# A gated linear recurrence with an ELU feed-forward layer: the state held per head and multiplied in four 64x64 quadrants

## The chip, the cores and the metric

The kernel runs on one core of a Trainium2 chip. The metric is the device time of one execution in microseconds (us). TensorE multiplies matrices into PSUM (eight banks of 512 fp32 columns on 128 partitions), VectorE and ScalarE work on SBUF and PSUM, GpSimd on SBUF alone, and SyncE (SP) issues the transfers. In the rows TensorE's matmuls are PE, its loads of the stationary operand PEld, VectorE DVE, ScalarE ACT and GpSimd POOL.

## The reference

Four sequences of 768 tokens, eight heads of 48 channels. A recurrence over tokens gives y; its heads side by side are x (3072 tokens, 384 channels), and two matrices with an ELU between them follow. Everything is fp32.

```python
B, H, S, D = r.shape                                  # 4, 8, 768, 48
for t in range(S):
    cur = np.einsum('bhd,bhe->bhde', u[None] * kt, vt)
    y[:, :, t] = np.einsum('bhd,bhde->bhe', rt, state + cur)
    state = w[None, :, :, None] * state + np.einsum('bhd,bhe->bhde', kt, vt)
x = y.transpose(0, 2, 1, 3).reshape(B * S, H * D)     # 3072 x 384
h = x @ w_in                                          # 384 x 2048
g = np.where(h > 0.0, h, np.exp(np.minimum(h, 0.0)) - 1.0)
out = g @ w_out                                       # 2048 x 384
```

## The kernel before

**Tiling.** The tokens of each sequence are cut into six chunks n of 128 (NCH). A unit is one (n, b), b being the sequence. The recurrence becomes matmuls per unit: the scores of the unit's tokens against each other for each head, masked; these by v; and the state left by the chunks before, by r. The state of b is then decayed and the chunk's k by v is added. Layer n is the feed-forward part for the 512 tokens of chunk n (all four b): 16 steps f, each with a hidden product (`hidden`, L939, 9 matmuls of 512 columns: three channel chunks by three products of high and low parts), the ELU over ScalarE and VectorE (L948, L949, L954), a split into high and low parts (L960, L962) and a projection of an earlier step (`project`, L976, 12 matmuls of 384 columns). The feed-forward products use fp32r operands, the recurrence fp32.

**Heads on partitions.** r and k, with channels on partitions, hold two heads on 128 partitions: the even head at rows 0 to 47, the odd one at 64 to 111 (ROWS), the other rows are padding. H / 2 = 4 such pairs a lie side by side (HP). `state[b]` has for each pair a 128x128 block of which only two 48x48 blocks, on the diagonal, are not zero.

**Order.** The order of the work is written out by hand and kept: START lists the start (chunk 0 and the first weights), FIRST the operations of one step of layer 0, LATER those of a step of layers 1 to 5. An operation's digit names the stage of the unit that it serves; a unit takes four steps. Layer 0 carries the units of chunk 1, layers 1 to 4 those of chunks 2 to 5, and layer 0 also prepares the weights (split into high and low parts on ScalarE, VectorE and GpSimd, L519 to L558). In layer 0 r and k are turned by TensorE (L567, then L621 on VectorE); from layer 1 on by VectorE's 32x32 transposes (L579) and two trips through DRAM (L588, L593), with L609 on GpSimd.

**What one unit does around the change.** `scores` (A, L692): 8 matmuls per head in row halves of the array (48 rows, 128 columns), odd and even heads into two banks, copied through a mask on VectorE by `take_scores` (L718). One step later `outputs` (Y): four state matmuls over whole pairs (L796, 128x128), eight matmuls of v by scores in column halves (L804, 64 columns), all into one bank y; right behind them `added_state` (L820), eight matmuls k by v of 48x48 into a second bank. `split_x` (xh on ScalarE, L847; xl on VectorE, L849) splits y into high and low parts: three of the four pairs go to x, the fourth to a tile `fill`, and `fill_x` (G, L858) moves its rows by six transfers into the padding rows of x, so that the 384 channels fill three chunks of 128. `new_state` (ns, L834) adds the added state to the decayed one, `decay_state` (sw on GpSimd, swd on VectorE in layer 0, L677) makes that decayed state, with one instruction for each half of the rows. PSUM: in the steps four banks hold the projection's sums, two the hidden product, and two in turn (tag rw) scores, y and added state.

**Channels.** Because of the padding x's channels are in another order than the reference's; `load_weights` (L212, L213) reads the rows of w_in in that same order, by two transfers for rows 0 to 47 and 64 to 111 and two for the padding rows. `x_tokens` (L763) and `turn_out` do the same for chunk 0, where y is computed with tokens on partitions.

Of the kernel before, what the change touches and what calls it, by code (L numbers as in the profile page):

```python
# [17 lines left out]
P = 128  # L18
B, H, S, D = 4, 8, 768, 48
DP = 64  # L20
# [6 lines left out]
X = 2 * NC * T  # L27

ROWS = [slice(i * DP, i * DP + D) for i in range(2)]
HALVES = [(rows, slice(None), rows) for rows in ROWS]  # L30


PAIR = 2 * D
REST = NC * PAIR
# [30 lines left out]
class Kernel:  # L65
# [7 lines left out]
    def prepare(self, ctx):  # L73
# [4 lines left out]
        self.state = [cp.tile([P, HP, P], F32, tag=f"state{b}", name=f"state{b}") for b in range(B)]  # L78
# [121 lines left out]
    def load_weights(self, j):  # L200
# [4 lines left out]
        if j % 2 == 0:  # L205

            st = st.rearrange("p (c f) t -> p c (f t)", c=NC)
            cols = slice(f * 2 * P, (f + 1) * 2 * P)
            pairs = self.w_in[0:REST, cols].rearrange("(c i p) f -> i p c f", c=NC, i=2)
            fill = self.w_in[REST:DM, cols].rearrange("(i c p) f -> i p c f", c=NC, i=2)  # L210
            for i in range(2):
                nc.sync.dma_start(st[ROWS[i]], pairs[i])  # L212
                nc.sync.dma_start(st[FILLS[i]], fill[i])  # L213
        else:
            nc.sync.dma_start(
                st.rearrange("p f t -> p (f t)"), self.w_out[f * P : (f + 1) * P, :]
            )
# [259 lines left out]
    def inverse_table(self):  # L477

        nc, wk = self.nc, self.wk
        near = wk.tile([P, HP, 16], F32, tag="near", name="near")  # L480
        far = wk.tile([P, HP, 8], F32, tag="far", name="far")
# [189 lines left out]
    def decay_state(self, n, b, eng=None):  # L671
# [4 lines left out]
        for at in HALVES:  # L676
            (eng or self.nc.gpsimd).tensor_mul(  # L677
                un["sw"][at[0]], self.state[b][at],
                self.pw[at[0], :, P : P + 1].to_broadcast([D, HP, D]),
            )  # L680
# [71 lines left out]
    def x_tokens(self, n, b):  # L752
# [5 lines left out]
        for part, at, form in (  # L758
            (slice(0, REST), slice(0, D), "p (c i d) -> p c i d"),
            (slice(REST, DM), slice(D, DP), "p (i c d) -> p c i d"),  # L760
        ):
            y_part, vd_part = (t[:, part].rearrange(form, c=NC, i=2) for t in (y, vd))
            nc.vector.tensor_add(x[:, :, :, at], y_part, vd_part)  # L763
# [10 lines left out]
    def x_of(self, n):  # L774
        if n not in self.x:
            self.x[n] = self.wk.tile(
                [P, 2, NC, T], F32R, tag="x", name="x", bufs=1 if self.general else 2
# [3 lines left out]
    def split_turned(self, n, b, i):  # L781
        nc, px = self.nc, self.units[n, b]["px"]
        x = self.x_of(n)[:, :, :, b * P : (b + 1) * P]
# [29 lines left out]
    def added_state(self, n, b):  # L813
# [4 lines left out]
        pst = self.bank("st")  # L818
        for h in range(H):
            nc.tensor.matmul(  # L820
                pst[ROWS[h % 2], (h // 2) * D : (h // 2 + 1) * D],
                lhsT=kr[:, h, 0:D], rhs=v_t[:, h, :], start=True, stop=True,
# [3 lines left out]
    def new_state(self, n, b):  # L826
# [5 lines left out]
        for at in HALVES:  # L832
            if n > 0:
                nc.vector.tensor_add(self.state[b][at], un["sw"][at[0]], un["ps"][at[0]])  # L834
            else:
                nc.scalar.copy(self.state[b][at], un["ps"][at[0]])
# [200 lines left out]
```

## Time and profile before

| | us |
|---|---|
| median of 3 runs | 528.35 (525.35 to 531.41) |
| the profiled execution's time | 524.89 |
| its span, first to last instruction | 523.1 |
| TensorE matmuls busy in the span | 504.1 |
| VectorE busy | 289.0 |
| ScalarE busy | 243.5 |
| GpSimd busy | 168.0 |

The profiled execution's time is 1.8 us over its span; it lies below the lowest of the three runs. Times in rows are microseconds from the span's start unless marked ns; L796 is line 796 of the kernel. A row of the timeline merges neighbouring instructions of one kind (x8): its length runs from the first one's start to the last one's end, and matmuls overlap, so that the distance between the starts of two rows says when TensorE goes on.

### The profile page before, as it was taken

The page shows a single profiled execution, that of the slowest core. Times are in us where ns is not written, and L with a number is a line of the kernel's source. Part 1 is how long each engine was busy: PE and PEld are TensorE (multiplying, and loading weights), DVE is VectorE, ACT ScalarE, POOL GpSimd, SP SyncE. Part 2 cuts the span into 40 slices and gives each one's busy share as a digit, 9 for nine tenths or more (in the row PEclk, how much of TensorE's full clock was granted, in tenths as well). Part 3 has the DMA queues.
Part 4 walks back from the last instruction along what each step waited for, and adds up shares of the span by engine and source line. Part 5 has one row for each costly group of instructions (what it writes and reads, how often), then busy time and mean ns, then how long its engine had stood idle before and what let it go on. Part 6 is the DMA issues. An engine that isn't in the chain of part 4 may idle for free.

```text
span 523.1 us, 9010 instructions
## 1 busy us (share of the span) xinstructions
PE 504.1 (96%) x3380; PEld 450.3 (86%) x3380; DVE 289.0 (55%) x496; ACT 243.5 (47%) x429; POOL 168.0 (32%) x192
## 2 busy tenths in 40 slices
PE   6889999999999999999999999999999999999994
PEld 5879898987988988988988988989889889999994
DVE  6989999996454454454444644544543542433331
ACT  2289787775344333434334443333434344444441
POOL 6732233125524524525525435234133220000000
PEclk9999999999999999999999999999999999999999
DMA  9987858535624523543424354335245200100001
GB/s 138 210 184 186 174 149 218 127 63 138 146 69 83 117 66 68 130 136 64 124 53 94 99 132 97 86 56 127 84 111 129 71 25 9 59 3 0 1 0 67
DMA packets 105561, 50.89 MB, mean 97 GB/s; under 512 B 80162, under 2 KB 101412, under 8 KB 105508
## 3 DMA queue, kind: packets, MB, share of 16 engines
q1 hardware_dynamic: 105508, 50.23, 42.0%
q8 instruction: 28, 0.46, 0.4%
q14 instruction: 25, 0.20, 0.1%
HBM read 35.13 MB, written 13.11 MB: 92 GB/s over the span
## 4 chain that ended last, share of the span: by engine, by line
PE 82%; DVE 6%; SPq 4%; ACT 3%; DMA 2%; issue 1%; POOL 0%; ACTq 0%; DVEq 0%
PE ps_acc L976 35%; PE ps_h L939 34%; PE ps_a L692 4%; PE ps_y L804 4%; PE ps_y L796 3%; DVE wide L541 1%; SPq L167 1%; PE ps_st L820 1%; DVE wide L533 1%; DVE rk L621 1%; ACT stage L525 1%; DVE ps_h L954 1%; DMA x<-fill 1%; PE ps_y L747 1%; SPq L212 1%
## 5 line engine op out<-in xcount | busy, mean ns | idle before, releaser
L976 PE MATMUL ps_acc<-wh,g 128*128 128x384 f32 x768 | 216.0, 343 | 0.5 <-DVE g L962 0.5
L939 PE MATMUL ps_h<-x,wh 128*128 128x512 f32 (+1 forms) x588 | 181.1, 389 | 0.7 <-DMA x<-fill 0.7
L976 PEld LDWEIGHTS ps_acc<-wh,g 128*128 128x128 f32 x768 | 139.9, 188 | 7.1 <-DVE g L962 1.0
L954 DVE SCALAR_TENSOR_TENSOR ps_h<-g,ps_h 128x512 f32<-128x512 f32 x96 | 66.8, 695 | 133.3 <-ACT g L949 132.8
L976 PE MATMUL ps_acc<-wl,g 128*128 128x384 f32 x384 | 129.0, 336 | 0.0
L939 PEld LDWEIGHTS ps_h<-x,wh 128*128 128x128 f32 x588 | 108.5, 188 | 16.9 <-DMA x<-fill 1.0
L948 ACT ACTIVATE g<-ps_h 128x512 f32<-128x512 f32 x96 | 57.4, 598 | 136.9 <-PE ps_h L939 136.9
L939 PE MATMUL ps_h<-x,wl 128*128 128x512 f32 (+1 forms) x294 | 114.1, 388 | 0.0
L960 ACT CAST g<-ps_h 128x512 fp32r<-128x512 f32 x96 | 56.4, 587 | 82.6 <-DVE ps_h L954 82.2
L962 DVE TENSOR_TENSOR g<-ps_h,g 128x512 fp32r<-128x512 f32 x96 | 66.0, 688 | 36.1 <-ACT g L960 35.2
L976 PEld LDWEIGHTS ps_acc<-wl,g 128*128 128x128 f32 x384 | 72.3, 188 | 1.9
L711 POOL TENSOR_TENSOR a<-ident,diag 128x512 f32<-128x512 f32 x35 | 35.9, 1045 | 108.6 <-DVE diag L660 100.7
L939 PEld LDWEIGHTS ps_h<-x,wl 128*128 128x128 f32 x294 | 55.1, 188 | 13.7
L949 ACT ACTIVATE g<-g 128x512 f32<-128x512 f32 x96 | 60.7, 632 | 3.1
L667 POOL TENSOR_TENSOR k_t<-k_t,rev 128x384 f32<-128x384 f32 x16 | 16.2, 1012 | 62.6 <-DVE tb L579 49.9
L558 POOL TENSOR_TENSOR wl<-wide,wh 128x384 fp32r<-128x384 f32 x17 | 17.4, 1021 | 50.5 <-ACT wh L551 46.1
L849 DVE TENSOR_TENSOR fill<-ps_y,fill 128x128 fp32r<-128x128 f32 x20 | 5.8, 290 | 46.7 <-ACT x L847 46.7
L718 DVE COPY_PREDICATED a<-mask,ps_a 128x512 f32<-128x512 int32 x40 | 27.3, 736 | 0.0
L652 POOL TENSOR_TENSOR ru<-r_t,u_b 128x384 f32<-128x384 f32 x17 | 17.3, 1016 | 17.4 <-DMA r_t<-in_r_dram 14.9
L796 PEld LDWEIGHTS ps_y<-rk,state 128*128 128x128 f32 x160 | 20.9, 191 | 1.6
L804 PE MATMUL ps_y<-a,v_t 128*64 128x128 f32 x320 | 21.9, 279 | 0.0
L609 POOL TENSOR_TENSOR rk<-rk,pw 128x512 f32<-128x512 f32 x16 | 19.1, 1192 | 6.6 <-DMA rk<-blocks 6.6
(105 smaller groups left out, 440.1 us busy)
## 6 DMA issues: line engine op xcount, KB each, us to landing
blocks<-tb SPq DMA_DIRECT2D x64, 128.0 KB, 2.3
rk<-blocks SPq DMA_DIRECT2D x16, 512.0 KB, 3.6
stage<-in_moe_w_out_dram SPq DMA_DIRECT2D x16, 384.0 KB, 4.2
stage<-in_moe_w_in_dram SPq DMA_DIRECT2D x32, 144.0 KB, 4.2
out_dram<-stage SPq DMA_DIRECT2D x24, 192.0 KB, 3.3
r_t<-in_r_dram SPq DMA_DIRECT2D x22, 192.0 KB, 3.4
k_t<-in_k_dram SPq DMA_DIRECT2D x22, 192.0 KB, 3.9
v_t<-in_v_dram SPq DMA_DIRECT2D x22, 192.0 KB, 4.1
```

The source lines that it names most:

```text
L692: self.nc.tensor.matmul(pa[i][:, a * P : (a + 1) * P], lhsT=kw[rows, a, :], rhs=rw[rows, a, :], start=True, stop=True,)
L711: self.nc.gpsimd.tensor_mul(un["a"][i], self.ident.unsqueeze(1).to_broadcast([P, HP, P]), diag.unsqueeze(2).to_broadcast([P, HP, P]),)
L718: self.nc.vector.copy_predicated(un["a"][i], self.mask.bitcast(I32).unsqueeze(1).to_broadcast([P, HP, P]), un["pa"][i].rearrange("p (a t) ...
L796: nc.tensor.matmul(py[:, a * P : (a + 1) * P], lhsT=self.state[b][:, a, :], rhs=un["r"][:, a, :], start=(a == 0), stop=False, skip_group_c ...
L804: nc.tensor.matmul(py[i * DP : (i + 1) * DP, a * P : (a + 1) * P], lhsT=v[:, h * D : h * D + DP], rhs=un["a"][i][:, a, :], start=(n == 0 a ...
L939: self.nc.tensor.matmul(ph[:, part], lhsT=a[:, c * P : (c + 1) * P], rhs=x[:, c, part], start=(c == 0 and i == 0), stop=(c == NC - 1 and i ...
L948: nc.scalar.activation(g, ph, AF.Relu, scale=-1.0)
L949: nc.scalar.activation(g, g, AF.Exp, scale=-1.0)
L954: self.nc.vector.scalar_tensor_tensor(ph, g, -1.0, ph, op0=ALU.add, op1=ALU.max)
L960: nc.scalar.copy(part, g)
L962: nc.vector.tensor_sub(part, g, self.g[n, f][2].bitcast(F32))
L976: self.nc.tensor.matmul(self.acc[n][b][:, 0:DM], lhsT=a[:, at], rhs=w, start=(f == 0 and i == 0), stop=(f == NF - 1 and i == 2),)
```

## The change

- `state[b]` keeps for each pair the two 48x48 blocks only: the even head's on rows 0 to 47, the odd head's on rows 64 to 111, both in the same 64 columns. Decay, addition and copies address those columns; the decay is one instruction over all partitions.
- `outputs` multiplies the state per head: eight matmuls of 48 rows by 64 columns instead of four of 128x128. Even heads (i = 0) read rows 0 to 47 and write bank py[0], odd heads rows 64 to 111 and py[1]; c = 0 or 1 picks partitions 0 to 63 or 64 to 127 of the bank. Heads run in the order s, i, c, with h = 4c + 2s + i. The matmuls of v by scores take the same order.
- y stands in the first 256 columns of two banks. The added state of chunks 1 to 4 goes to the last 256 columns of py[0], no longer to a bank of its own.
- x's channel chunk k (k = 0 to 3) is head k on rows 0 to 63 and head 4 + k on rows 64 to 127; `split_x` copies two chunks from each bank, 256 columns at a time. The tile x has room for chunk 3, which took the tile `fill` before; `fill_x` reads it there. The rows of w_in, `x_tokens` and the split of chunk 0 follow that order. The tiles near and far of the start lie in the tile sw.

```diff
-        self.state = [cp.tile([P, HP, P], F32, tag=f"state{b}", name=f"state{b}") for b in range(B)]
+        self.state = [cp.tile([P, HP, DP], F32, tag=f"state{b}", name=f"state{b}") for b in range(B)]
...
-            pairs = self.w_in[0:REST, cols].rearrange("(c i p) f -> i p c f", c=NC, i=2)
-            fill = self.w_in[REST:DM, cols].rearrange("(i c p) f -> i p c f", c=NC, i=2)
+            heads = self.w_in[:, cols].rearrange("(i c p) f -> i p c f", i=2, p=D)
             for i in range(2):
-                nc.sync.dma_start(st[ROWS[i]], pairs[i])
-                nc.sync.dma_start(st[FILLS[i]], fill[i])
+                last = slice((i * HP + NC) * D, (i + 1) * HP * D)
+                fill = self.w_in[last, cols].rearrange("(c p) f -> p c f", c=NC)
+                nc.sync.dma_start(st[ROWS[i]], heads[i][:, 0:NC])
+                nc.sync.dma_start(st[FILLS[i]], fill)
...
         un["sw"] = self.wk.tile([P, HP, D], F32, tag="sw", name="sw", bufs=1)
-        for at in HALVES:
-            (eng or self.nc.gpsimd).tensor_mul(
-                un["sw"][at[0]], self.state[b][at],
-                self.pw[at[0], :, P : P + 1].to_broadcast([D, HP, D]),
-            )
+        (eng or self.nc.gpsimd).tensor_mul(
+            un["sw"], self.state[b][:, :, 0:D], self.pw[:, :, P : P + 1].to_broadcast([P, HP, D])
+        )
...
     def outputs(self, n, b):
         nc, un = self.nc, self.units[n, b]
         v = self.raw[n, b][2]
-        py = self.bank("y")
+        py = un["py"] = [self.bank("y") for _ in range(2)]
+        at = [
+            (4 * c + 2 * s + i, py[i][c * DP : (c + 1) * DP, s * P : (s + 1) * P], s)
+            for s in range(2) for i in range(2) for c in range(2)
+        ]
         if n > 0:
-            for a in range(HP):
+            for h, y, s in at:
+                rows, a = ROWS[h % 2], h // 2
                 nc.tensor.matmul(
-                    py[:, a * P : (a + 1) * P], lhsT=self.state[b][:, a, :], rhs=un["r"][:, a, :],
-                    start=(a == 0), stop=False, skip_group_check=True,
+                    y, lhsT=self.state[b][rows, a, :], rhs=un["r"][rows, a, :],
+                    start=(s == 0), stop=False, skip_group_check=True,
                 )
-        for h in range(H):
-            a, i = h // 2, h % 2
+        for h, y, s in at:
             nc.tensor.matmul(
-                py[i * DP : (i + 1) * DP, a * P : (a + 1) * P], lhsT=v[:, h * D : h * D + DP],
-                rhs=un["a"][i][:, a, :], start=(n == 0 and a == 0), stop=(a == HP - 1),
-                skip_group_check=True,
-            )
-        un["py"] = py.rearrange("p (c t) -> p c t", c=HP)
+                y, lhsT=v[:, h * D : h * D + DP], rhs=un["a"][h % 2][:, h // 2, :],
+                start=(n == 0 and s == 0), stop=(s == 1), skip_group_check=True,
+            )
...
-        pst = self.bank("st")
+        pst = (self.bank("st") if n == 0 else un["py"][0])[:, 2 * P :]
...
     def split_x(self, n, b, i):
         nc, un = self.nc, self.units[n, b]
-        if "fill" not in un:
-            un["fill"] = self.wk.tile([P, 2, P], F32R, tag="fill", name="fill", bufs=2)
-        x, fill, py = self.x_of(n)[:, :, :, b * P : (b + 1) * P], un["fill"], un["py"]
-        for hi, lo, y in (
-            (fill[:, 0], fill[:, 1], py[:, NC]), (x[:, 0], x[:, 1], py[:, 0:NC])
-        ):
+        for j, py in enumerate(un["py"]):
+            x = self.x_of(n)[:, :, j::2, b * P : (b + 1) * P]
+            y = py[:, 0 : 2 * P].rearrange("p (s t) -> p s t", s=2)
             if i == 0:
-                nc.scalar.copy(hi, y)
+                nc.scalar.copy(x[:, 0], y)
             else:
-                nc.vector.tensor_sub(lo, y, hi.bitcast(F32))
+                nc.vector.tensor_sub(x[:, 1], y, x[:, 0].bitcast(F32))
...
-                self.nc.sync.dma_start(x[FILLS[i], :, c], fill[rows])
+                self.nc.sync.dma_start(x[FILLS[i], :, c], x[rows, :, NC])
```

## Rows read from the trace of the kernel before

**Rows 1.** The page: TensorE's busy time, its 40 slices and its granted clock.
```profile
PE 504.1 (96%) x3380; PEld 450.3 (86%) x3380; DVE 289.0 (55%) x496; ACT 243.5 (47%) x429; POOL 168.0 (32%) x192
...
PE   6889999999999999999999999999999999999994
...
PEclk9999999999999999999999999999999999999999
```

**Rows 2.** Busy by stage: length, PE, PEld, DVE, ACT, POOL (instructions), clock, DMA, GB/s.
```profile
39.00:122.00 83.00, 78.94 (x555) 70.08 (x555) 76.25 (x126) 65.76 (x115) 24.10 (x24) 1.00 0.64 151
122.00:204.00 82.00, 82.00 (x561) 72.85 (x563) 40.91 (x71) 32.96 (x60) 37.66 (x41) 1.00 0.46 103
...
367.00:434.00 67.00, 67.00 (x428) 59.65 (x429) 30.52 (x51) 27.55 (x49) 17.56 (x16) 1.00 0.32 82
```

**Rows 3.** TensorE's waits from 38 us on: total us, times, longest.
```profile
PE ps_a L692 <- DVE rk L621: 4.0, 4, 1.3
...
PEld ps_a L692 <- issue: 4.9, 14, 0.4
```

**Rows 4.** Timeline of TensorE over a unit in layer 2: start, length, instruction, tiles.
```profile
223.85 0.39 PE L939 MATMUL ps_h<-x,wl 128*128 128x512 f32 x1
224.17 1.16 PE L692 MATMUL ps_a<-rk,tb 48*128 48x128 f32 x16
225.26 0.45 PE L976 MATMUL ps_acc<-wh,g 128*128 128x384 f32 x1
...
228.61 0.40 PE L939 MATMUL ps_h<-x,wl 128*128 128x512 f32 x1
...
229.30 0.39 PE L939 MATMUL ps_h<-x,wl 128*128 128x512 f32 x1
229.53 1.05 PE L796 MATMUL ps_y<-rk,state 128*128 128x128 f32 x8
230.51 1.09 PE L804 MATMUL ps_y<-a,v_t 128*64 128x128 f32 x16
231.44 0.53 PE L820 MATMUL ps_st<-v_t,k_t 128*48 128x48 f32 x16
...
244.58 0.38 PE L692 MATMUL ps_a<-rk,tb 48*128 48x128 f32 x2
```

**Rows 5.** TensorE's timeline in windows 224.165:224.178 and 230.512:230.530: records begun.
```profile
224.17 0.38 PE L692 MATMUL ps_a<-rk,tb 48*128 48x128 f32 x2
...
230.51 0.33 PE L804 MATMUL ps_y<-a,v_t 128*64 128x128 f32 x2
```

**Rows 6.** Groups by line and shape: count, busy us, mean ns, idle before, releasers.
```profile
L796 PE MATMUL ps_y<-rk,state 128*128 128x128 f32 x160 | 21.0, 274 | 0.0
...
L847 ACT CAST x<-ps_y 128x384 fp32r<-128x384 f32 x20 | 9.7, 486 | 0.0
...
L849 DVE TENSOR_TENSOR fill<-ps_y,fill 128x128 fp32r<-128x128 f32 x20 | 5.8, 290 | 46.7 <-ACT x L847 46.7
L847 ACT CAST fill<-ps_y 128x128 fp32r<-128x128 f32 x20 | 5.3, 266 | 16.3 <-PE ps_y L804 13.9 <-PE ps_st L820 2.3
...
L677 DVE TENSOR_TENSOR sw<-state,pw 48x192 f32<-48x192 f32 x8 | 3.3, 411 | 0.1
```

**Rows 7.** Timeline of a unit in layer 0, from its state product on.
```profile
66.76 1.05 PE L796 MATMUL ps_y<-rk,state 128*128 128x128 f32 x8
...
68.91 0.27 ACT L847 CAST fill<-ps_y 128x128 fp32r<-128x128 f32 x1 [1.25 <-PE ps_st L820]
...
70.75 0.70 DVE L954 SCALAR_TENSOR_TENSOR ps_h<-g,ps_h 128x512 f32<-128x512 f32 x1 [0.21 <-ACT g L949]
```

**Rows 8.** Timeline of the end of layer 0.
```profile
114.48 0.73 DVE L677 TENSOR_TENSOR sw<-state,pw 48x192 f32<-48x192 f32 x2
...
117.58 0.55 DVE L849 TENSOR_TENSOR x<-ps_y,x 128x384 fp32r<-128x384 f32 x1
...
121.97 0.73 PE L939 MATMUL ps_h<-x,wh 128*128 128x512 f32 x2 [0.73 <-DMA x<-fill]
```

More of the change, by code (lines that the diff above doesn't have):

```diff
@@ L26 @@
 T = B * P
-X = 2 * NC * T
+X = 2 * (NC + 1) * T
 ROWS = [slice(i * DP, i * DP + D) for i in range(2)]
-HALVES = [(rows, slice(None), rows) for rows in ROWS]
-PAIR = 2 * D
-REST = NC * PAIR
 FILL = DP - D
@@ L479, in inverse_table @@
         nc, wk = self.nc, self.wk
-        near = wk.tile([P, HP, 16], F32, tag="near", name="near")
-        far = wk.tile([P, HP, 8], F32, tag="far", name="far")
+        t = wk.tile([P, HP, D], F32, tag="sw", name="near", bufs=1)
+        near, far = t[:, :, 0:16], t[:, :, 16:24]
         nc.vector.reciprocal(near, self.pw[:, :, 1:17])
@@ L757, in x_tokens @@
         y, vd = un["py"][:, 0:DM], un["vd"].rearrange("p h d -> p (h d)")
-        for part, at, form in (
-            (slice(0, REST), slice(0, D), "p (c i d) -> p c i d"),
-            (slice(REST, DM), slice(D, DP), "p (i c d) -> p c i d"),
-        ):
-            y_part, vd_part = (t[:, part].rearrange(form, c=NC, i=2) for t in (y, vd))
-            nc.vector.tensor_add(x[:, :, :, at], y_part, vd_part)
+        y, vd = (t.rearrange("p (i c d) -> p c i d", i=2, d=D) for t in (y, vd))
+        nc.vector.tensor_add(x[:, :, :, 0:D], y[:, 0:NC], vd[:, 0:NC])
+        y, vd = (t[:, NC].rearrange("p i (c d) -> p c i d", c=NC) for t in (y, vd))
+        nc.vector.tensor_add(x[:, :, :, D:DP], y, vd)
     def turn_out(self, n, b):
@@ L776, in x_of @@
             self.x[n] = self.wk.tile(
-                [P, 2, NC, T], F32R, tag="x", name="x", bufs=1 if self.general else 2
+                [P, 2, NC + 1, T], F32R, tag="x", name="x", bufs=1 if self.general else 2
             )
@@ L782, in split_turned @@
         nc, px = self.nc, self.units[n, b]["px"]
-        x = self.x_of(n)[:, :, :, b * P : (b + 1) * P]
+        x = self.x_of(n)[:, :, 0:NC, b * P : (b + 1) * P]
         if i == 0:
@@ L821, in added_state @@
                 pst[ROWS[h % 2], (h // 2) * D : (h // 2 + 1) * D],
-                lhsT=kr[:, h, 0:D], rhs=v_t[:, h, :], start=True, stop=True,
+                lhsT=kr[:, h, 0:D], rhs=v_t[:, h, :], start=True, stop=True, skip_group_check=True,
             )
@@ L831, in new_state @@
             self.added_state(n, b)
-        for at in HALVES:
+        for rows in ROWS:
+            state = self.state[b][rows, :, 0:D]
             if n > 0:
-                nc.vector.tensor_add(self.state[b][at], un["sw"][at[0]], un["ps"][at[0]])
+                nc.vector.tensor_add(state, un["sw"][rows], un["ps"][rows])
             else:
-                nc.scalar.copy(self.state[b][at], un["ps"][at[0]])
+                nc.scalar.copy(state, un["ps"][rows])
     def split_x(self, n, b, i):
         nc, un = self.nc, self.units[n, b]
-        if "fill" not in un:
-            un["fill"] = self.wk.tile([P, 2, P], F32R, tag="fill", name="fill", bufs=2)
-        x, fill, py = self.x_of(n)[:, :, :, b * P : (b + 1) * P], un["fill"], un["py"]
-        for hi, lo, y in (
-            (fill[:, 0], fill[:, 1], py[:, NC]), (x[:, 0], x[:, 1], py[:, 0:NC])
-        ):
+        for j, py in enumerate(un["py"]):
+            x = self.x_of(n)[:, :, j::2, b * P : (b + 1) * P]
+            y = py[:, 0 : 2 * P].rearrange("p (s t) -> p s t", s=2)
             if i == 0:
-                nc.scalar.copy(hi, y)
+                nc.scalar.copy(x[:, 0], y)
             else:
-                nc.vector.tensor_sub(lo, y, hi.bitcast(F32))
+                nc.vector.tensor_sub(x[:, 1], y, x[:, 0].bitcast(F32))
     def fill_x(self, n, b):
         x = self.x[n].bitcast(F32)[:, :, :, b * P : (b + 1) * P]
-        fill = self.units[n, b]["fill"].bitcast(F32)
         for i in range(2):
```

## The prediction

> **What bounds the kernel now.** I read the page's busy shares and its 40 slices first, to see which engine is full and for how long. TensorE is busy 96% of the span, at 9 tenths or more from the fourth slice on, at the upper of its two clock levels throughout [rows 1]. The table by stage then splits this. The start ends near 39 us. Layer 0 runs to 122 us: TensorE has 78.94 of 83 us, but VectorE is nearly as full with 76.25. From 122 to 434 us, where the last unit ends, TensorE has every microsecond (82.00 of 82 at first, 67.00 of 67 at last, the stages between alike) and VectorE half of them [rows 2]. The waits say the same: apart from the 0.3 to 0.4 us ahead of the scores' matmuls (L692), put down to "issue", TensorE waits for another engine almost only in layer 0, for the VectorE product L621 [rows 3]. So in those stages a microsecond less on TensorE is a microsecond less of the span, and in layer 0 it has to be asked what else stands in the chain.
>
> **A unit, record by record.** A unit is one (chunk n, batch b); 20 of them (n = 1 to 5) have a state product, four with their second half in layer 0 and 16 in layers 1 to 4. The timeline of TensorE over one of the 16 [rows 4] gives all prices. Each fp32 matmul leaves two records: four state matmuls (L796) make x8 here and x160 in all [rows 6].
> - The last L939 record begins at 229.30, the first of L796 at 229.53: 0.23 us, the ordinary pace of L939 (228.61 to 229.30 are three records). Entering L796 costs nothing.
> - L796: eight records in 1.05 us, the last one 0.275 long, so (1.05 - 0.27) / 7 = 0.11 us apart. L804 starts 0.98 us after L796: eight paces are 0.89, the other 0.09 is the price of going from 128x128 to 128x64.
> - L804 uses two column halves in turn: 16 records, 0.93 us to L820's first. At 0.11 us for each PAIR that is 0.88, plus 0.05 at its front. So two column halves run at once.
> - L692 uses two row halves: it starts 0.32 us after the last L939 record (0.09 over the ordinary 0.23) and L976 follows after 1.09: eight pairs at 0.11 are 0.89, so 0.20 for its front and for leaving the form.
> Narrow windows confirm the pairs: in one of 13 ns two records of L692 have begun, in one of 18 ns two of L804 [rows 5].
>
> **The change, part by part.**
> *The state product.* Before: eight records one after another. After: per head, 48 rows by 64 columns, eight matmuls, 16 records, in four quadrants. No row shows four quadrants at once. Lower bound: all four run together, 16 / 4 = 4 paces. Upper bound: only two run together, as in either half-form, 8 paces. I take 4: quadrants read as many values per partition and pass as L804's two halves, and write as many banks and partitions as L692's two halves, and each of these runs at full pace by itself; the two row halves now write to two banks, as L692's do. Price after, from the end of L939: 0.09 (entry, by L692) + 0.05 (front, by L804, the same 64-column load) + 4 x 0.11 + 0.02 (an estimate for four starts instead of two; the two of a pair are under 13 ns apart [rows 5]) + 0.09 (exit, by L796) = 0.69 us. Against 0.98 that saves 0.29 us a unit. If entry and exit were free it would be 0.47; if the front cost twice L692's 0.10 and each switch 0.15, it would be 0.98 - 0.96 = 0.02.
> *Layers 1 to 4.* 16 x 0.29 = 4.6 us. Nothing else comes in between: VectorE and GpSimd are idle half the time there [rows 2], and of the 20.4 us of a unit (L692 at 224.17 and 244.58 [rows 4]) only 0.29 goes.
> *Outputs (L804) and added state (L820).* Same number, forms and alternation of column halves; only order and banks differ. 0. The second y bank takes the place of the state's: two banks a unit, as before. It has to be free before the state product rather than before L820, but the scores it replaces are already waited for by L804. 0, and at most one pass of L718 if that were late.
> *The bank that y and the added state now share.* ScalarE's first copy of y (L847) must follow the last L820 matmul, if banks are kept apart between engines. The trace speaks for that: VectorE's subtraction for the fill (L849) waits 46.7 us in all for ScalarE's copy of the OTHER columns of that bank [rows 6]. The copy begins 0.08 us after L804's end in layer 0 (66.76 + 0.98 + 1.09 = 68.83, then 68.91) [rows 7]. After: 66.76 + 0.69 + 0.93 + 0.53 (L820) + 0.08 = 68.99. So what TensorE gains is given back, and 0.08 us more. In layers 1 to 4 the copy has time: TensorE needs its result with the next chunk's first hidden product, over two steps later. In layer 0 it is in the chain: behind it on ScalarE stand L948 and L949, and VectorE's L954 waits for them, 0.21 us, right after [rows 7]; from there the chain goes through ScalarE and VectorE to L621, for which the next scores wait. So units 1 to 3 of layer 0 give +0.08 each, 0.2 us lost. Without that wait the copy starts at 66.76 + 0.69 + 1.09 + 0.08 = 68.62, 0.29 us earlier, 0.9 us gained over three units.
> *Copies and subtractions of y.* ScalarE 128x128 (266 ns) and 128x384 (486) become twice 128x256, by interpolation 2 x 376; the sum is the same [rows 6]. VectorE likewise. 0.
> *Decayed state (L677).* Two 48-partition products become one over 128 partitions with the same 192 columns: on VectorE (layer 0 only) one of 411 ns goes [rows 6], 0.36 us of the pair's 0.73. In units 1 to 3 it falls ahead of a wait for ScalarE and gives nothing. In the last one VectorE runs without a break from L677 (114.48) to the last subtraction (117.58), the fill transfers follow that, and TensorE waits 0.73 us for them at 121.97 [rows 8]: there 0.36 us come through. On GpSimd it shortens an engine with time to spare. 0.
> *Fill transfers (L858), weights' loads (L212).* The same number and size on SP's queue, only other rows; the source is x itself. They still wait for the last subtraction. 0.
> *Start.* Halved clearing of the state on GpSimd, the same number of copies and transposes: 0, with up to 0.5 us either way.
> Sum: -4.6 + 0.2 - 0.36 = -4.8 us. The profiled execution took 524.89 us (span 523.1 and 1.8 around it), so 520.1; from the median of the runs shown, 528.35, it is 523.5. I predict 523.5 us, 0.9% less.
>
> **A rule against it.** The narrow windows show two records of L692 on the way within 13 ns [rows 5], although the two records of one matmul, on the same half, cannot overlap (L796 keeps them 0.11 us apart). So the second record of one head does not hold up the first of the next. The Trainium skill, "TensorE: Matmul & The Clock Gate", Part 3, What overlaps and what doesn't, states that matmuls start and end in strict program order. If the program holds both passes of a head next to each other, that rule would let only the second pass of one head run beside the first of the next. What it would do here is rival 2 below.
>
> **Rivals.**
> 1. *Four quadrants run, and less is lost around them.* Either ScalarE's copy does not wait for L820 (0.29 us earlier in three units: -4.6 - 0.9 - 0.36 = -5.9, 522.5 us), or a switch between tiled forms is cheaper than one from the full array (0.09 less a unit: -1.4 more, 522.1). Against the first: the fill's 46.7 us. Chance 0.2.
> 2. *Slower: no more than two run at once.* Eight paces in place of four: 0.69 + 0.44 = 1.13 a unit, 0.15 more than before. 16 x 0.15 = 2.4; in layer 0 the copy starts 0.52 us later than now, 3 x 0.52 = 1.6; less 0.36: +3.6, 532 us. With passes strictly in order nine paces: 1.24, +0.26 a unit, 4.2 + 1.9 - 0.4 = +5.7, 534.1 us. It decides from 6.6 paces on, where 0.25 + 6.6 x 0.11 is the old 0.98: when fewer than 2.4 quadrants (16 / 6.6) overlap on the mean. For it: no row has four at once. Against it: rows 5. Chance 0.1.
> 3. *Part of the overlap.* Second passes that wait take up the place from which the next quadrant would be served; then 16 records take some 5.5 paces, 0.85 us, a gain of 0.13: -2.1, +0.7 in layer 0, -0.36: -1.8, 526.6 us. Chance 0.15.
> 4. *The gain is hidden*, because TensorE is not what ends last in layers 1 to 4. The table by stage speaks against it: 82.00 of 82 us. 528. Chance 0.05.
>
> **How the numbers follow.** My forecast, 523.5 (its own range 522 to 525.5), has 0.5; rivals 1 to 4 have 0.2, 0.1, 0.15 and 0.05. About 1% (5.3 us) is what a measurement of this kernel can tell from no change. The forecast lies just inside, so a third of it (0.17) and most of rival 1 (0.15) are faster by over 1%: 0.32. Slower by over 1% is the strict order alone and some of rival 2: 0.06. Within 1%: 0.62. The range goes from 519.5 (rival 1 with both, and the median's own scatter) to 530.0, short of rival 2.
>
> **What would show it.** Of the state product: x16 records, about 0.60 us from its first start to L804's, and 0.09 more ahead of it; four records begun within some 25 ns. A pace of 0.11 for two says rival 2. A unit of 20.12 us in place of 20.41 in layers 1 to 4; in layer 0 units as long as before, with ScalarE's first copy right behind L820. One VectorE product of some 0.4 us for L677. If the unit of layers 1 to 4 does not shrink by what the state product loses, the forecast's main step is wrong.

## The result and the profile after

The changed kernel takes 523.41 us (median of 19 runs, 521.1 to 527.78) against 528.35 for the kernel before (19 runs, 525.11 to 531.61): a ratio of 0.9911, 95% interval 0.9888 to 0.9934. Predicted were 523.5 us. The profiled execution took 522.45 us with a span of 520.5 (before 524.89 and 523.1). That is only 2.4 us less; where the rest of the distance between the medians comes from is told below.

The page of the kernel after: TensorE's busy time and its granted clock, beside [rows 1].

```profile
PE 501.3 (96%) x3540; PEld 441.3 (85%) x3540; DVE 286.6 (55%) x492; ACT 243.6 (47%) x429; POOL 160.9 (31%) x180
...
PEclk9999999999999999999999999999999999999999
```

TensorE has 160 matmul records more and is busy 2.8 us less. In the table by stage (columns as in [rows 2]) it still fills the stages of layers 1 to 4, apart from the wait at the end of layer 0. One of them:

```profile
204.00:286.00 82.00, 82.00 (x611) 72.24 (x610) 40.45 (x71) 33.48 (x60) 31.95 (x32) 1.00 0.40 95
```

The unit of [rows 4] in the kernel after, from TensorE's timeline. L687 is now the scores, L932 hidden, L796 the state product, L802 the matmuls of v by scores, L816 the added state, L969 the projection:

```profile
223.87 1.16 PE L687 MATMUL ps_a<-rk,tb 48*128 48x128 f32 x16
...
229.00 0.40 PE L932 MATMUL ps_h<-x,wl 128*128 128x512 f32 x1
229.33 0.67 PE L796 MATMUL ps_y<-rk,state 48*64 48x128 f32 x16
229.93 1.09 PE L802 MATMUL ps_y<-a,v_t 128*64 128x128 f32 x16
...
244.02 0.49 PE L687 MATMUL ps_a<-rk,tb 48*128 48x128 f32 x4
```

From the last L932 record to L802 it is 229.93 - 229.00 = 0.93 us, of which 0.23 are L932's own pace, so 0.70 for the state product; before it was 0.98. From score to score the unit is 244.02 - 223.87 = 20.15 us; before 20.41. How the 16 records of 0.67 us are made shows in the same timeline cut to the 23 ns from 229.330 to 229.353:

```profile
229.33 0.34 PE L796 MATMUL ps_y<-rk,state 48*64 48x128 f32 x4
```

Four records begin in it. The groups by line of the kernel after (columns as in [rows 6]; L841 are ScalarE's copies of y, L843 VectorE's subtractions):

```profile
L796 PE MATMUL ps_y<-rk,state 48*64 48x128 f32 x320 | 13.8, 282 | 0.2 <-DVE a L713 0.2
...
L843 DVE TENSOR_TENSOR x<-ps_y,x 128x256 fp32r<-128x256 f32 x40 | 15.1, 418 | 41.2 <-ACT x L841 41.2
L841 ACT CAST x<-ps_y 128x256 fp32r<-128x256 f32 x40 | 13.0, 376 | 15.2 <-PE ps_y L816 14.5 <-PE ps_y L802 0.6
```

ScalarE's copies now wait for the added state (L816, 14.5 us in all) instead of y's own matmuls (L804, 13.9 in [rows 6]).

**Where the time went.** I measure every kernel by the starts of the scores' matmuls on TensorE. "Units of layer 0" are the three distances between the first four, "the last piece" is the distance from the fourth to the first in layer 1, and "the unit" is the mean of the 15 distances between the 16 units of layers 1 to 4 (it is a little under the unit seen above, because four of the 15 distances are shorter in every kernel: one in layer 1 is 18.31 us before and 18.09 after, the last three are 20.04 and 19.78).

| us | first scores | units of layer 0 | last piece | unit, mean of 15 |
|---|---|---|---|---|
| before | 39.13 | 22.26, 22.28, 22.28 | 18.28 | 20.195 |
| before again (e4_before) | 41.36 | 22.27, 22.28, 22.28 | 18.27 | 20.195 |
| after | 39.22 | 23.09, 22.29, 22.29 | 18.33 | 19.936 |
| after again (e1_again) | 41.34 | 22.38, 22.29, 22.29 | 17.75 | 19.935 |
| after again (e9_again5) | 45.97 | 22.40, 22.31, 22.29 | 17.82 | 19.936 |
| second bank split first (e2_py1_first) | 42.15 | 22.07, 22.02, 22.01 | 18.22 | 19.936 |
| the same (e10_py1_5) | 42.21 | 22.08, 22.01, 22.01 | 17.81 | 19.937 |
| by quadrant (e3_by_quadrant) | 39.34 | 22.42, 22.31, 22.33 | 17.97 | 19.956 |
| row halves (e5_row_halves) | 41.39 | 22.99, 22.89, 22.90 | 17.80 | 20.529 |
| two products (e6_two_products) | 45.97 | 22.43, 22.31, 22.30 | 18.27 | 19.936 |
| state product twice (e7_twice) | 38.90 | 22.84, 22.74, 22.74 | 17.80 | 20.369 |
| no state product (e8_no_state) | 39.26 | 22.10, 21.70, 21.70 | 17.78 | 19.339 |

The unit repeats to 0.002 us, and 15 x (20.195 - 19.936) = 3.9 us is the gain of layers 1 to 4. What moves from one profile of a kernel to the next is the start, the first unit of layer 0 and the last piece.

The state product lost 0.28 us or a little more, the unit only 0.26. Where the rest goes shows best in layer 5, which carries no unit. From the start of one projection to that of the second one after it, kernel before:

```profile
447.11 0.34 PE L976 MATMUL ps_acc<-wh,g 128*128 128x384 f32 x1
...
455.43 0.34 PE L976 MATMUL ps_acc<-wh,g 128*128 128x384 f32 x1
```

The same in the kernel after:

```profile
443.95 0.34 PE L969 MATMUL ps_acc<-wh,g 128*128 128x384 f32 x1
...
452.30 0.34 PE L969 MATMUL ps_acc<-wh,g 128*128 128x384 f32 x1
```

These two steps of the feed-forward part take 8.35 us instead of 8.32, with the same matmuls. The version without a state product (e8_no_state, below) has it too, so it is not the state product; which other part of the change does it was not tried. It adds up: from the last unit's scores to the start of the last matmul it is 515.58 - 427.15 = 88.43 us before and 512.66 - 424.25 = 88.41 after, although the sixteenth state product lies in that stretch. So the 3.9 us are all that is gained behind layer 0.

### The profile page after: what moved, and what is told of

It reads as the page before. It is cut to its first block, busy times and chain, and to the rows that moved or that the text cites. A ratio compares the mean times of both kernels' runs of the same rounds, so it can differ in the third digit from the quotient of the medians.

```text
span 520.5 us, 9232 instructions
## 1 busy us (share of the span) xinstructions
PE 501.3 (96%) x3540; PEld 441.3 (85%) x3540; DVE 286.6 (55%) x492; ACT 243.6 (47%) x429; POOL 160.9 (31%) x180
## 4 chain that ended last, share of the span: by engine, by line
PE 79%; DVE 6%; ACT 5%; SPq 5%; DMA 2%; issue 1%; POOL 0%; ACTq 0%; DVEq 0%; POOLq 0%
PE ps_acc L969 35%; PE ps_h L932 33%; PE ps_a L687 4%; PE ps_y L802 4%; PE ps_y L796 2%; ACT stage L522 1%; DMA stage<-in_moe_w_in_dram 1%; SPq L163 1%; DVE wide L538 1%; DVE wide L530 1%; PE ps_y L816 1%; ACT stage L516 1%; SPq L167 1%; DVE ps_h L947 1%; SPq L209 1%
## 5 line engine op out<-in xcount | busy, mean ns | idle before, releaser
L969 PE MATMUL ps_acc<-wh,g 128*128 128x384 f32 x768 | 216.6, 343 | 0.3 <-DVE g L955 0.2
L932 PE MATMUL ps_h<-x,wh 128*128 128x512 f32 (+1 forms) x588 | 180.2, 388 | 1.3 <-DMA x<-x 1.3
L969 PEld LDWEIGHTS ps_acc<-wh,g 128*128 128x128 f32 x768 | 140.1, 187 | 7.0 <-DVE g L955 0.9
L969 PE MATMUL ps_acc<-wl,g 128*128 128x384 f32 x384 | 129.3, 337 | 0.0
L932 PEld LDWEIGHTS ps_h<-x,wh 128*128 128x128 f32 x588 | 108.1, 188 | 18.0 <-DMA x<-x 1.6
L932 PE MATMUL ps_h<-x,wl 128*128 128x512 f32 (+1 forms) x294 | 114.1, 388 | 0.0
L969 PEld LDWEIGHTS ps_acc<-wl,g 128*128 128x128 f32 x384 | 72.1, 188 | 2.1
L932 PEld LDWEIGHTS ps_h<-x,wl 128*128 128x128 f32 x294 | 55.2, 188 | 11.7
L843 DVE TENSOR_TENSOR x<-ps_y,x 128x256 fp32r<-128x256 f32 x40 | 15.1, 418 | 41.2 <-ACT x L841 41.2
L713 DVE COPY_PREDICATED a<-mask,ps_a 128x512 f32<-128x512 int32 x40 | 27.0, 727 | 0.0
L802 PE MATMUL ps_y<-a,v_t 128*64 128x128 f32 x320 | 21.9, 279 | 0.0
L606 POOL TENSOR_TENSOR tb<-rk,qw 128x512 f32<-128x512 f32 x16 | 20.7, 1296 | 0.0
```

The source lines that it names most:

```text
L606: self.nc.gpsimd.tensor_mul(dst, src, by)
L713: self.nc.vector.copy_predicated(un["a"][i], self.mask.bitcast(I32).unsqueeze(1).to_broadcast([P, HP, P]), un["pa"][i].rearrange("p (a t) ...
L802: nc.tensor.matmul(y, lhsT=v[:, h * D : h * D + DP], rhs=un["a"][h % 2][:, h // 2, :], start=(n == 0 and s == 0), stop=(s == 1), skip_grou ...
L932: self.nc.tensor.matmul(ph[:, part], lhsT=a[:, c * P : (c + 1) * P], rhs=x[:, c, part], start=(c == 0 and i == 0), stop=(c == NC - 1 and i ...
L969: self.nc.tensor.matmul(self.acc[n][b][:, 0:DM], lhsT=a[:, at], rhs=w, start=(f == 0 and i == 0), stop=(f == NF - 1 and i == 2),)
```

## The experiments

**After and before once more.** The first profile of the kernel after lost 0.9 us in layer 0 against before. Is that the change, or the execution? Both kernels were run again, unedited.

> The changed kernel once more, unedited, for a second profile. Theory (the gain is that of the 16 units in layers 1 to 4, and start and layer 0 only scatter): a unit of layers 1 to 4 again 20.14 to 20.15 us between its scores against 20.41 before, 3.9 us over the 15 distances; from the first scores to the fifth within 1 us of the 85.10 of the kernel before; time 0.989 to 0.993 of before. Rival (layer 0 really is longer by 0.9 us, as in the first profile after): first to fifth scores again 85.9 to 86.1 us, with the first unit longer than 23 us again.

> The kernel before once more, for a second profile. Theory: a unit of layers 1 to 4 again 20.41 us; first to fifth scores 85.1 us give or take 1 us, so that a difference of 0.9 us in layer 0 between two single profiles says nothing of the change. Rival: 85.1 again to 0.1 us, so that the 0.9 us are the change's.

Measured: e1_again 524.37 us (521.12 to 528.55), ratio 0.9959, interval 0.9912 to 1.0007, so above the 0.989 to 0.993 expected, and its interval includes no change (only one of its ten executions had a mean granted clock of 0.995 or more; see the last section); e4_before, one execution, 527.37 us. In the table the kernel before is the same to 0.01 us behind the start, while the first unit of after is 22.38 instead of 23.09 and the last piece 17.75 instead of 18.33. From the first scores to those of layer 1 it is 85.10 us in both profiles of before, which was the rival's sign, but 84.72 in e1_again, where the rival wanted 85.9 or more. So the 0.9 us came with that execution: without it layer 0 is 0.38 us shorter than before, not longer. The end of layer 0, kernel after, first profile (SPq are SP's issues of transfers; in brackets the idle time ahead and what ended it):

```profile
113.41 3.31 SPq L585 DMA_DIRECT2D blocks<-tb  x4
...
117.79 0.75 DVE L843 TENSOR_TENSOR x<-ps_y,x 128x256 fp32r<-128x256 f32 x2
118.70 0.34 SPq L590 DMA_DIRECT2D rk<-blocks  x1
119.15 3.79 SPq L851 DMA_DIRECT2D x<-x  x6
...
122.94 0.73 PE L932 MATMUL ps_h<-x,wh 128*128 128x512 f32 x2 [1.29 <-DMA x<-x]
```

The same stretch in e1_again:

```profile
114.81 2.37 SPq L585 DMA_DIRECT2D blocks<-tb  x4
...
119.15 0.34 SPq L590 DMA_DIRECT2D rk<-blocks  x1
119.20 0.74 DVE L843 TENSOR_TENSOR x<-ps_y,x 128x256 fp32r<-128x256 f32 x2
120.01 3.79 SPq L851 DMA_DIRECT2D x<-x  x6
...
123.79 0.50 PE L932 MATMUL ps_h<-x,wh 128*128 128x512 f32 x1 [0.72 <-DMA x<-x]
```

In e1_again the fill transfers (L851) are issued 0.07 us after the last subtraction ends (119.20 + 0.74). In the first profile they come 0.61 us after it, because SP's four issues L585 took 3.31 us instead of 2.37 and pushed L590 and L851 back; TensorE waits 1.29 us instead of 0.72. Why an issue takes 1 us longer in one execution stays open. The kernel before has such slow issues too, but not here: its four took 1.78 us at this place and 3.13 at another (208.93 us).

The other part of the 0.9 us lies in the first unit. In the first profile VectorE stood idle for 0.90 us ahead of a product of the weights (L530, 41.12 us), which it did not in e1_again. Its masked copies of the scores (L713) ended late by that, and the state product had to stop for them:

```profile
44.76 0.44 PE L796 MATMUL ps_y<-rk,state 48*64 48x128 f32 x4
45.38 0.65 PE L796 MATMUL ps_y<-rk,state 48*64 48x128 f32 x12 [0.18 <-DVE a L713]
```

From its first start to L802 (45.97 us) it took 1.21 us instead of 0.60; in e1_again it runs without a stop. L713 reads the scores' bank, and y's second bank takes the place of scores in the changed kernel; so a late masked copy holds up the state product already, and not only the matmuls of v by scores behind it. That would be a price of the change; no run undoes it.

**Does ScalarE's copy wait for the added state in the same bank, and does layer 0 hang on it?** The bank without added state is split first.

```diff
-        for j, py in enumerate(un["py"]):
+        for j, py in reversed(list(enumerate(un["py"]))):
```

> Only the order of the two copies and of the two subtractions of y is turned: the bank without the added state first. Theory (ScalarE's first copy waits for the added state in its bank, and in layer 0 the chain runs over that copy): the first copy begins some 0.1 us after the outputs' last matmul instead of after the added state's, 0.36 us earlier; units of layer 0 22.0 us instead of 22.29, about 1 us less in all; layers 1 to 4 unchanged at 20.14 to 20.15. Rival (the copy is not in the chain of layer 0, VectorE alone sets it): the copy starts earlier all the same, units of layer 0 stay at 22.29, time as the changed kernel's.

Measured: 522.69 us (519.85 to 523.61), ratio 0.99, interval 0.9858 to 0.9941. The units of layer 0 fall from 22.29 to 22.02 and 22.01, those of layers 1 to 4 stay. A unit of layer 0, kernel after:

```profile
69.27 0.53 PE L816 MATMUL ps_y<-v_t,k_t 128*48 128x48 f32 x16
69.84 0.65 ACT L841 CAST x<-ps_y 128x256 fp32r<-128x256 f32 x2 [1.26 <-PE ps_y L816]
```

The same in e2_py1_first:

```profile
71.20 0.53 PE L816 MATMUL ps_y<-v_t,k_t 128*48 128x48 f32 x16
71.44 0.70 ACT L841 CAST x<-ps_y 128x256 fp32r<-128x256 f32 x2 [0.93 <-PE ps_y L802]
```

From the start of L816 to the copy it is 0.57 us in one and 0.24 in the other, and what ended the wait is L816 in one and L802 in the other. The copy is 0.33 us earlier, the unit 0.27 shorter. Both halves of the theory hold. The Trainium skill, "PSUM — Partial Sum Buffer", PSUM bank collisions raise a hardware error, says that the compiler's scheduler makes one instruction wait for another on a different engine where both touch one bank and the same 32 partitions, and that a different address there still collides. The trace agrees: copy and added state share partitions and bank, not columns, and the wait of 1.26 us ends with L816.

**Do quadrants take their matmuls independently?** In the changed kernel neighbouring matmuls go to different quadrants. Here the two of one quadrant stand next to each other.

```diff
-            for h, y, s in at:
+            for h, y, s in sorted(at, key=lambda t: (t[0] % 2, t[0] // 4, t[2])):
```

> Only the order of the eight state matmuls is changed: the two of one quadrant behind each other, then the next quadrant's, so that four records of one quadrant stand ahead of the first of the next. Theory (each quadrant takes its own records from a queue, waiting ones of another quadrant do not hold them up): again 0.60 us from the first state record to the outputs' first, time as the changed kernel's. Rival (TensorE serves only a few records ahead in program order, so neighbours overlap and no more): 0.60 grows to between 1.0 (two quadrants overlap) and 1.9 us (none does), 6 to 21 us more over 16 units.

Measured: 524.37 us (521.59 to 528.11), ratio 0.9938, interval 0.9895 to 0.9981. The state product of e3_by_quadrant, with the next row behind it:

```profile
228.58 0.69 PE L796 MATMUL ps_y<-rk,state 48*64 48x128 f32 x16
229.20 1.09 PE L802 MATMUL ps_y<-a,v_t 128*64 128x128 f32 x16
```

0.62 us from its first start to L802, 0.02 more than in the order of the change (0.60), and a unit 0.02 longer. Four records of one quadrant stand ahead of the next quadrant's first, and hardly hold it up. The timeline of e3_by_quadrant cut to 228.584 to 228.740 has four begun, within the first 41 ns, and then no fifth:

```profile
228.58 0.36 PE L796 MATMUL ps_y<-rk,state 48*64 48x128 f32 x4
```

No row says on which quadrant a record runs. But in all forms here as many records start in each pace of 0.11 us as the form has blocks (one on the full array, two in halves, four in quadrants), which says that those of one block start 0.11 us apart. Then strict program order would have taken 13 paces of 0.11 us, 1.4 us in place of 0.62, and starts are not in strict program order across quadrants. The Trainium skill, "TensorE: Matmul & The Clock Gate", Part 3, What overlaps and what doesn't, states that matmuls start and end in strict program order; the measurement decides against it here.

**Is it four at once that gains, or the split into two banks?** The product per head on row halves, 128 columns wide. Eight matmuls and two banks as after, but only two halves of the array.

```diff
-                    y, lhsT=self.state[b][rows, a, :], rhs=un["r"][rows, a, :],
-                    start=(s == 0), stop=False, skip_group_check=True,
+                    py[h % 2][:, s * P : (s + 1) * P],
+                    lhsT=self.state[b][rows, 2 * s : 2 * s + 2, :].rearrange("p a d -> p (a d)"),
+                    rhs=un["r"][rows, a, :],
+                    start=(s == 0 and h < 4), stop=False, skip_group_check=True,
```

> The state product of the changed kernel in two row halves instead of four quadrants: the same eight matmuls and 16 records, each with 128 stationary columns (two heads' states side by side) and 128 output partitions, so that y also gets another head's product. Theory (what counts is how many records run at once): eight paces of 0.11 us and 0.10 for loading 128 columns in front, so 0.10 + 0.89 + 0.09 = 1.08 us from the first state record to the outputs' first instead of 0.60, a unit of 20.63 us instead of 20.15. Rival (a quadrant product saves by its smaller blocks, not by running four at once): well under 1.0 us.

Measured, one execution: 534.34 us. State product of e5_row_halves:

```profile
235.03 1.26 PE L796 MATMUL ps_y<-rk,state 48*128 48x128 f32 x16
236.22 1.09 PE L804 MATMUL ps_y<-a,v_t 128*64 128x128 f32 x16
```

1.19 us, one pace more than the 1.08 expected. The front is as expected: 0.21 us from the first pair's starts to the second's, a pace and 0.10. The pace is lost further back, where two of the 16 records start alone, so that they take nine steps. One of them is the last, as the timeline cut to 236.185 to 236.215 shows:

```profile
236.02 0.27 PE L796 MATMUL ps_y<-rk,state 48*128 48x128 f32 x1
```

In this version two matmuls of the same half stand next to each other in the program; whether that costs the pace was not tried. The unit is 20.53 in the mean, 0.33 over that of before, and without the lost pace still 0.22 over it. So the form per head with only two at once would have made the kernel slower. Its blocks are also twice as wide as those of the quadrants, but a pace is 0.11 us in both; the gain is that of four at once.

**One VectorE product less at the end of layer 0.** The decayed state in two instructions again, in the new layout.

```diff
-        (eng or self.nc.gpsimd).tensor_mul(
-            un["sw"], self.state[b][:, :, 0:D], self.pw[:, :, P : P + 1].to_broadcast([P, HP, D])
-        )
+        for rows in ROWS:
+            (eng or self.nc.gpsimd).tensor_mul(
+                un["sw"][rows], self.state[b][rows, :, 0:D],
+                self.pw[rows, :, P : P + 1].to_broadcast([D, HP, D]),
+            )
```

> Only the decayed state is made by two 48-partition products again instead of one over 128. Theory (VectorE's stretch ahead of the fill transfers at the end of layer 0 is the one place where it counts): two products take 0.73 to 0.86 us instead of 0.35 to 0.53 us; scores four to five of layer 0 some 0.36 us longer, where no slow issue of a transfer hides it (17.75 us in the second profile of the changed kernel); units one to three of layer 0 unchanged at 22.3; layers 1 to 4 unchanged at 20.15 although GpSimd has 0.5 us more a unit. Rival (GpSimd or VectorE set the units): units longer by 0.3 to 0.5 us.

Measured, one execution: 528.08 us. Its partner is e9_again5, which has the same start to 0.01 us. End of layer 0 in e6_two_products:

```profile
124.40 0.75 DVE L845 TENSOR_TENSOR x<-ps_y,x 128x256 fp32r<-128x256 f32 x2
...
124.75 0.34 SPq L590 DMA_DIRECT2D rk<-blocks  x1
...
125.21 3.15 SPq L853 DMA_DIRECT2D x<-x  x5
```

In e9_again5:

```profile
123.88 0.75 DVE L843 TENSOR_TENSOR x<-ps_y,x 128x256 fp32r<-128x256 f32 x2
...
124.27 0.34 SPq L590 DMA_DIRECT2D rk<-blocks  x1
...
124.72 3.79 SPq L851 DMA_DIRECT2D x<-x  x6
```

In e9_again5 the fill transfers go 0.49 us earlier, and the last piece is 0.45 us shorter (18.27 to 17.82). But this pair does not isolate the product. SP's four issues L585 took 3.23 us in e6_two_products and 2.79 in e9_again5, so L590 is 0.48 us earlier as well, and in both the fill transfers follow L590 after 0.45 or 0.46 us, so that SP alone could make the difference.

A better pair is the first profile of before and e1_again, where SP waits for VectorE's last subtraction. SP's waits there (us in all, times, longest), before and then e1_again:

```profile
SPq L858 <- DVE x L849: 1.3, 1, 1.3
```

```profile
SPq L851 <- DVE x L843: 0.5, 1, 0.5
```

VectorE's next instruction behind the two products of the kernel before, which start at 114.48 [rows 8]:

```profile
115.25 0.56 DVE L558 TENSOR_TENSOR wl<-wide,wh 128x384 fp32r<-128x384 f32 x1
```

The one product of e1_again and the same next instruction:

```profile
116.80 0.35 DVE L673 TENSOR_TENSOR sw<-state,pw 128x192 f32<-128x192 f32 x1
117.07 0.55 DVE L555 TENSOR_TENSOR wl<-wide,wh 128x384 fp32r<-128x384 f32 x1
```

From start to start that is 0.77 us and 0.27, so 0.50 less. The fill transfers come 0.06 and 0.07 us behind the last subtraction, and the last piece is 0.53 us shorter (18.28 to 17.75). So the product counts where SP is on time; where its issues are slow, as in the first profile of after (18.33), nothing of it is seen. Units of layers 1 to 4, where GpSimd has the products, stay at 19.936 in e6_two_products.

**Is TensorE all that a unit waits for?** Once with the state product done twice, once without it.

```diff
-            for h, y, s in at:
+            for h, y, s in at + at:
```

```diff
-        if n > 0:
+        if False:
...
-                start=(n == 0 and s == 0), stop=(s == 1), skip_group_check=True,
+                start=(s == 0), stop=(s == 1), skip_group_check=True,
```

> Every state matmul is made twice (the second time over the first). Theory: four paces of 0.11 us more a unit, 1.04 us from the first state record to the outputs' first; a unit of layers 1 to 4 20.59 us, 7.0 us over 16; in layer 0 the copies of y come 0.44 us later and units are 22.7 us, 1.3 us over three; in all 8 us more than the changed kernel, about 1.006 to 1.009 of before. Rival (layer 0 follows VectorE, not the copy of y): layer 0 unchanged, 7 us more. Rival (other engines set the units of layers 1 to 4): less than 7 us.

> The state product is left out, so y lacks the part of the chunks before. Theory: of the 0.69 us only the way into the outputs' form (0.09) stays, so 0.60 us less a unit: 19.55 us in layers 1 to 4, 9.6 us over 16; in layer 0 up to 0.6 us less a unit as long as the copy of y is in the chain; in all 10 to 11.5 us less than the changed kernel, about 0.97 of before. Rival (layer 0 has a second chain right behind, VectorE's): units of layer 0 not under 22.0 us.

Measured: e7_twice 528.94 us (528.41 to 529.46), ratio 1.0021, interval 0.9988 to 1.0053; e8_no_state 511.63 us (509.65 to 512.3), ratio 0.9688, interval 0.9622 to 0.9755. The doubled product:

```profile
231.29 1.10 PE L796 MATMUL ps_y<-rk,state 48*64 48x128 f32 x32
232.33 1.09 PE L802 MATMUL ps_y<-a,v_t 128*64 128x128 f32 x16
```

1.04 us instead of 0.60, so 0.44 more; the unit is 0.433 longer. Without the product it is 0.597 shorter. What TensorE gains or loses in layers 1 to 4 is what the unit gains or loses. Units of layer 0 move by +0.45 and -0.59: the chain through ScalarE's copy follows TensorE there as well. The ratio of e7_twice lies below the 1.006 to 1.009 expected. All its executions were at a granted clock of 0.995 or more; against executions of before at the same granted clock (last section) it is 528.94 / 525.18 = 1.007.

**Two versions side by side.** The changed kernel and the one that splits the second bank first.

> The changed kernel again, for a direct comparison with the version that splits the second bank first. Units of layers 1 to 4 at 20.14 us, units of layer 0 at 22.29 us as in both profiles so far. Theory (the state product sets the units of layers 1 to 4; what differs between profiles is the start and the places where an issue is slow): a ratio between 0.990 and 0.995 to the kernel before. If the third transfer of the blocks of the last unit of layer 0 is issued in about 1 us, the last piece of layer 0 is 17.75 us; if it takes about 2 us, about 18.3.

> The second bank of y (which holds no added state) is split first. Theory: each of the three first units of layer 0 is 22.02 us instead of 22.29, layers 1 to 4 as in the changed kernel, so 0.8 us less than the changed kernel in the same comparison, a ratio 0.0015 lower. Rival (what layer 0 gains there is lost again at its end): the distance from the first scores to those of layer 1 is that of the changed kernel, and the ratios are equal.

Measured: e9_again5 521.9 us (520.63 to 528.05), ratio 0.9912, interval 0.9879 to 0.9946; e10_py1_5 520.69 us (520.35 to 523.01), ratio 0.9867, interval 0.9822 to 0.9911. From the first scores to those of layer 1 it is 84.82 us in one and 83.91 in the other, so nothing of the 0.27 us a unit is lost again. Against before the second version is clearly faster. Against the changed kernel it has 0.9 us for it in the trace; the two intervals overlap. Among executions at a mean granted clock of 0.995 or more it is 0.9 us too: 521.60 (7 executions) and 520.67 (6). In e9_again5 the last piece is 17.82 us, close to the 17.75 that was expected with quick issues, with L585 at 2.79 us.

## Why the prediction was right, step by step

- **The state product, four paces.** Predicted 0.69 us from the end of L932, measured 0.70; four records within 23 ns where under 25 was said; 0.10 ahead of the first start (0.09 predicted). All three prices (entry, front, pace) held. Rivals 2 and 3 fall by that, the strict order by e3_by_quadrant also, if the records of one quadrant start 0.11 us apart. e5_row_halves shows that rival 2 had the right consequence: two at once is slower than before, by 0.33 us a unit where 0.15 was worked out (the front costs 0.05 more with 128 columns than with the 64 of the sum, and one pace was lost).
- **Layers 1 to 4, slope one.** Right: e7_twice and e8_no_state. Rival 4 falls.
- **16 x 0.29 = 4.6 us.** Too much by 0.7 us. The block lost 0.28 to 0.29 us, but the unit only 0.26, so it is 3.9 us over 15 distances, and what the sixteenth gains is used up behind it. The step that was off is "Nothing else comes in between": 0.03 us are lost again in two steps of the hidden product and the projection (8.35 instead of 8.32 us), in layer 5 too. What in the change does that stays open.
- **The copy waits for the added state.** Right, and shown by undoing it (e2_py1_first). The first half of rival 1 falls with it, the second (a cheaper switch) with the 0.10 us of the entry. Predicted was +0.08 us for each of the units 1 to 3 of layer 0. Measured is +0.12 for the first and +0.01 for the other two (e1_again; +0.14, +0.03 and +0.01 in e9_again5), so the sum of 0.2 us came out nearly (0.14 and 0.18) but not by equal shares. In units 2 and 3 the copy begins 0.04 us after the last L816 record's end (69.27 + 0.53, then 69.84) instead of 0.08; why the first unit pays more is not shown.
- **End of layer 0.** Mechanism right where SP is on time (before against e1_again), size 0.50 to 0.53 us instead of 0.36: the sum took the difference of two lengths, but the records overlap, and what counts is the distance between starts. The prediction left out that SP's issues can end last there; in the first profile of after they did and hid the gain.
- **Nothing elsewhere.** Layer 0 as a whole: +0.2 - 0.36 = -0.16 us predicted, -0.38 and -0.28 measured (84.72 and 84.82 against 85.10, e1_again and e9_again5), but +0.9 in the first profile. There the wait came that the prediction put at "at most one pass of L718": the state product of the first unit stood for its bank, 0.6 us in all.
- **From the sum to the time.** Terms from the traces: -3.9 - 0.3 = -4.2 us with layer 0 as in the two later profiles, -3.8 with the mean of all three, where -4.8 were predicted. The medians differ by 4.9 us; that this comes so near to the prediction is partly luck, by the mix of executions. Taking only those whose mean granted clock was 0.995 or more, before is 525.18 us (22 executions) and after 521.54 (8; in e9_again5 521.60, 7): 3.6 us. Such executions of the kernel before still range over 1.6 us (524.45 to 526.04), so 3.6 and 4.2 are not at odds; which of them is closer isn't settled.

## What to carry to other kernels

Where TensorE is full, a block-diagonal product over whole pairs was cheaper here as blocks of its own in four quadrants (0.70 us instead of 0.98 a unit), and its price can be read ahead from rows of half-forms: pace, front and entry add up. But the split paid only because all four run at once; with two at once it cost more than the full array did. Price an instruction by the distance between starts and not by its length: the product saved at the end of layer 0 was worth 0.50 us and not 0.36. When two results share a bank, ask which engine reads it first: splitting the bank that is not written any more first gave 0.27 us a unit where the reader was in the chain.

## What the hardware showed beyond that

**The scatter is the clock in the start.** Executions of one kernel differ by 6 us and more, and what differs is where the first scores come (39.2 to 46.0 us in the table for the changed kernel). Granted clock over the start in the table by stage (columns as in [rows 2]), kernel after, first profile:

```profile
20.00:23.00 3.00, 2.69 (x39) 2.42 (x38) 3.00 (x7) 1.06 (x2) 1.49 (x2) 1.00 1.15 206
23.00:39.00 16.00, 13.27 (x155) 11.85 (x151) 13.86 (x25) 10.98 (x21) 7.49 (x7) 1.00 0.83 174
```

The same kernel in e9_again5:

```profile
20.00:23.00 3.00, 1.97 (x20) 1.71 (x21) 3.00 (x8) 0.48 (x1) 1.91 (x2) 0.98 1.23 204
23.00:39.00 16.00, 15.87 (x120) 14.98 (x120) 10.32 (x21) 6.92 (x13) 5.49 (x5) 0.50 0.57 107
```

From 23 to 39 us TensorE was granted 0.50 of the full clock, its lower level of 1.2 GHz; it did 120 matmul records in that time instead of 155, and the first scores came at 45.97 us instead of 39.22. What stood ahead of the fall shows in TensorE's timeline (in brackets the idle time). Kernel after, first profile:

```profile
20.73 0.52 PE L762 MATMUL ps_xT<-ident,x_f 128*128 128x128 f32 x3 [0.31 <-DVE rk L618]
```

The same place in e9_again5:

```profile
21.95 0.52 PE L762 MATMUL ps_xT<-ident,x_f 128*128 128x128 f32 x3 [1.03 <-DVE rk L618]
```

TensorE had stood idle for 1.03 us instead of 0.31. But an idle stretch of that length isn't needed: in e10_py1_5 the clock was down as well, from 26 to 36 us, with TensorE busy for 2.36 of the 3 us ahead of it (table by stage). In the first profile of the kernel after it was busy for 2.35 of the same 3 us, and the clock stayed at 1.00. e10_py1_5:

```profile
23.00:26.00 3.00, 2.36 (x19) 2.12 (x19) 2.57 (x4) 0.87 (x2) 3.00 (x3) 0.98 0.78 200
26.00:36.00 10.00, 9.88 (x81) 9.12 (x82) 6.72 (x14) 5.60 (x13) 2.28 (x3) 0.50 0.63 123
```

The kernel before pays it too: its executions at a mean clock of 0.995 or more have a median of 525.18 us, the 33 others 528.28. For a change worth 4 us this scatter is as large as the effect, and the distances between marks in the trace, which repeat to 0.002 us a unit, tell more than the medians. What makes the clock fall in one execution and not in the next was not tried.
